# A stack of softmax attention and linear attention on one core: VectorE's exponential by two quadratics, two rings for 4 KB tiles, and an attention order found by looking ahead

## The chip, the core and the metric

The kernel runs on one core of a Trainium2 chip. The core has TensorE (PE, matrix products into the accumulator memory PSUM), VectorE (DVE), ScalarE (ACT), GpSimd (POOL) and SyncE (SP, whose queue issues most DMA transfers). The engines run on their own instruction queues, each in order, and wait for each other by semaphores. Times are device microseconds (us) of the core. The time before is the median of 3 runs, 2476.19 us (2473.14 to 2482.28). A difference under some 0.5% cannot be told from no change.

## The reference, cut to what matters

Four residual layers of 2048 tokens by 512 channels, 32 heads of 16 channels: softmax attention A, linear attention B, and the two again with the same weights.

```python
def _A_ref(x, wqkv, wo):
    qkv = (x @ wqkv).reshape(B, S, 3, H, Dh).transpose(2, 0, 3, 1, 4)
    q, k, v = qkv[0], qkv[1], qkv[2]
    scores = jnp.einsum("bhqd,bhkd->bhqk", q, k) * (Dh ** -0.5)
    p = _softmax(scores, axis=-1)
    o = jnp.einsum("bhqk,bhkd->bhqd", p, v)
    return o.transpose(0, 2, 1, 3).reshape(B, S, D) @ wo

def _B_ref(x, wqkv, w_phi, wo):        # q, k, v as above
    pq, pk = (jnp.einsum("bhsd,hdf->bhsf", t, w_phi) for t in (q, k))
    phi_q, phi_k = (concatenate([_softmax(p), _softmax(-p)], axis=-1) for p in (pq, pk))
    kv, z = jnp.einsum("bhsf,bhsd->bhfd", phi_k, v), jnp.einsum("bhsf->bhf", phi_k)
    o = jnp.einsum("bhqf,bhfd->bhqd", phi_q, kv) / (jnp.einsum("bhqf,bhf->bhq", phi_q, z)[..., None] + 1e-6)
    return o.transpose(0, 2, 1, 3).reshape(B, S, D) @ wo

x = A_x                                  # (1, 2048, 512)
for _ in range(2):
    x = x + _A_ref(_layernorm(x), A_wqkv, A_wo)
    x = x + _B_ref(_layernorm(x), B_wqkv, B_w_phi, B_wo)
```

## The kernel before, in words

*Tiling of attention.* The 32 heads are 8 sets of 4, the 2048 queries 4 blocks of 512; a set and a block are a group G, 32 groups in a layer. A group runs over 16 key tiles of 128 keys. For a key tile and two of the four heads, TensorE computes one score tile of 128 keys by 1024 values (`score_cols`, L1277, 8 matmuls of 49 rows). ScalarE takes the exponential of the whole tile (`scores`, L1284) into an SBUF tile `p` of 4 KB a partition. Two such tiles make a step, and TensorE multiplies them with the values (`pvs`, L1327, 8 matmuls in 32 bits, each profiled as two instructions, over 512 queries, or in two halves of 256). That is 1024 score tiles and 512 steps of P times V in an attention. In PSUM there are two double buffers `s` for ScalarE's tiles; a third double buffer (`double`) and a pair of single ones (`pm`) serve everything else, and one of these two always holds the group's accumulator.

*Power tiles.* Some score tiles get their exponential on VectorE instead (`power_task`). The score goes to `double` or `pm`. For each half of 512 values VectorE evacuates it in two instructions (L1295, L1298: the power of two and the rest), shifts the exponent into place (L1304), squares the rest (L1307) and evaluates a polynomial in four steps (L1309, L1311, L1313, L1315). The result is a tile `px`, of which there is one buffer, so one power tile is in flight.

*Side work.* Between score tiles and P times V, TensorE also makes the next heads' keys, queries and values (`octet`, units of 8 matmuls at L724), the output projection (`part`, `tail`), and in the first attention it prepares the weights of B. VectorE evacuates these (`kq_task`: L1011, L1013, L1016, L1019, L1021; transposes at L985; residual sums at L1361), GpSimd adds, squares (L1108) and subtracts. Query blocks that are done are normalized for the next layer while attention still runs (`stats_task`, L586; `halved`, L609 and L614).

*What sets the order.* `attention` is a planner that runs when the kernel is built. It keeps a clock for TensorE (`pe`) and one for ScalarE (`act`), costs such as 0.217 for a score tile and 0.864 for a step, and times at which buffers come free; tasks of VectorE and GpSimd stand in a list with their own clocks (`Plan`). At each turn it issues a score tile if a buffer `s` is free, else a side unit, else a P times V if a margin allows, else a power tile. The margins come from a table `RULES`, three numbers for each 32 steps. A power tile is aimed 8 steps ahead (`LEAD`) and starts if VectorE's planned work ends within 0.4 us (`VBUSY`). Loads by SP's queue are taken as landed after fixed times (`LAND`, 36 us).

*Buffers.* Tiles of 4 KB: 6 for `p` and 1 for `px` (pool `pp`); 3 `xt` for blocks that DMA loads or stores, and 4 tiles `xn` of 2 KB for normalized rows and the power tile's steps (pool `xp`).

*Layer B.* While the first rows come out of attention's end, B's `feed` projects each 128 tokens, and VectorE takes maximum, minimum, differences and sums of the feature maps (L1717 to L1731). Then `flow`, a second list planner, interleaves B's outputs with the start of the next attention.

## Time and profile before

| what | us |
|---|---|
| median of 3 runs | 2476.2 |
| the profiled execution's span | 2479.1 |
| before the first exponential | 71 |
| first attention | 935 |
| first B: feed, then outputs and the next projections | 168 + 132 |
| second attention | 923 |
| second B: feed, then outputs | 167 + 83 |
| busy: PE, ACT, DVE, POOL | 2307, 2122, 1641, 531 |

The profiled execution has no other time of its own than its span, which is 2.9 us above the median. In a row of groups stand line, engine, operation, output and inputs, shape and count; then busy time in all, the mean of one in ns, and the engine's idle time just before with who ended it. A row of waits gives the one who waited, the one waited for, and then us in all, times, and the longest. A row of a stretch gives its bounds and length, and for each engine its busy us with the number of instructions. A row of the timeline starts with the start and the length. PE's matmuls are pipelined, so the next one starts before the row's length is over.

### The profile page before, as it was taken

Reading aid. Unit: us, or ns where it says so; the run is one execution under the profiler, and the core shown is the slowest. Engines: PE = TensorE matmul, PEld = TensorE weight load, DVE = VectorE, ACT = ScalarE, POOL = GpSimd, SP = SyncE. Lnnn points to the kernel's source line nnn. Section 1 sums busy time; section 2 is a strip of 40 time slices with the busy share of each in tenths; the row PEclk is TensorE's granted clock in tenths of the full one; section 3 lists DMA queues with packets and bytes.
Section 4 is the critical chain, followed back from the end, with each engine's and each line's share of the span. In section 5 each row is a group of like instructions: output and inputs, shape, how many; then the busy total and the mean of one; then the engine's idle time right before and its main releaser. Section 6 shows DMA issues by size and latency. Waiting matters only on the chain.

```text
span 2479.1 us, 110386 instructions
## 1 busy us (share of the span) xinstructions
...
## 2 busy tenths in 40 slices
...
GB/s 193 71 28 8 88 72 37 30 59 55 37 55 155 140 75 67 44 35 18 60 73 57 40 8 63 34 3 53 66 21 42 97 78 43 71 71 26 27 1 112
DMA packets 124025, 143.31 MB, mean 58 GB/s; under 512 B 65193, under 2 KB 70937, under 8 KB 122649
## 3 DMA queue, kind: packets, MB, share of 16 engines
...
q14 instruction: 87, 0.70, 0.1%
...
## 4 chain that ended last, share of the span: by engine, by line
ACT 56%; PE 15%; DVE 13%; issue 12%; POOL 2%; SPq 1%; DMA 1%; POOLq 0%; ACTq 0%; DVEq 0%
ACT p L1284 55%; PE s L1277 3%; PE pm L1327 3%; PE double L1327 1%; PE pbv L1655 1%; DVE su L1728 1%; PE pk L1655 1%; DVE yt L1945 1%; PE pq L1655 1%; PE double L724 1%; DVE f L1720 1%; POOL f L1737 1%; DVE f L1721 1%; SPq L999 1%; DVE mx L1717 1%
## 5 line engine op out<-in xcount | busy, mean ns | idle before, releaser
L1284 ACT ACTIVATE p<-s 128x1024 f32<-128x1024 f32 x1998 | 1838.3, 1077 | 25.1 <-PE s L1277 23.6
L1277 PE MATMUL s<-kq 49*32 49x512 f16 x15104 | 793.4, 382 | 81.4 <-ACT p L1284 61.5
L1327 PE MATMUL pm<-p,v 64*32 64x512 f32 (+1 forms) x13216 | 805.5, 534 | 2.8 <-issue 2.8
L1277 PEld LDWEIGHTS <-kq 49*32 49x32 f16 x15872 | 388.8, 89 | 804.4 <-issue 704.8
L1327 PE MATMUL double<-p,v 64*32 64x512 f32 (+1 forms) x5848 | 320.6, 491 | 0.0
L1327 PEld LDWEIGHTS pm<-p,v 64*32 64x32 f32 x13216 | 262.2, 106 | 42.9 <-issue 7.3
L988 POOL TENSOR_TENSOR yt<-yt,yt 128x512 f32<-128x512 f32 x64 | 85.0, 1327 | 847.2 <-DVE yt L985 822.6
L985 DVE STREAM_TRANSPOSE yt<-pm 128x512 f32<-128x512 f32 x92 | 60.5, 695 | 207.4 <-PE pm L1327 207.4
L1655 PEld LDWEIGHTS <-xnTa 128*128 128x128 f16 x1152 | 111.0, 99 | 155.2 <-DVE f L1721 27.1
L1108 POOL TENSOR_TENSOR sq<-stg 128x512 bf16<-128x512 f16 x48 | 57.2, 1192 | 427.0 <-PE s L1277 266.3
L1737 POOL TENSOR_TENSOR f<-f,su 128x1024 f32<-128x1024 f32 x58 | 112.1, 1933 | 115.7 <-DVE su L1731 103.0
L1327 PEld LDWEIGHTS double<-p,v 64*32 64x32 f32 x5848 | 116.5, 106 | 21.1 <-issue 3.2
L1655 PE MATMUL pbv<-wbv,xnTa 128*128 128x512 f16 x384 | 92.8, 393 | 22.3 <-DVE f L1721 22.3
L1722 ACT ACTIVATE f<-f,c_pB 128x1024 f32<-128x1024 f32 x62 | 70.5, 1148 | 48.2 <-DVE f L1721 48.1
L1011 DVE TENSOR_SCALAR tq<-double,c_qk 128x512 f32<-128x512 f32 x36 | 26.8, 745 | 116.0 <-PE double L724 111.3
L724 PEld LDWEIGHTS <-wA 64*32 64x32 f16 x4608 | 75.5, 93 | 42.4 <-issue 3.6
L1361 DVE SCALAR_TENSOR_TENSOR xt<-pm,c_oA,xt 128x512 f32<-128x512 f32 x56 | 41.8, 746 | 80.5 <-PE pm L724 78.1
L1743 ACT ACTIVATE fk<-f 128x1024 f16<-128x1024 f32 x30 | 31.7, 1057 | 72.5 <-POOL f L1737 72.5
L985 DVE STREAM_TRANSPOSE vyt<-double 128x512 f32<-128x512 f32 x48 | 31.5, 692 | 87.9 <-PE double L724 84.7
L1655 PE MATMUL pq<-wbqk,xnTa 128*128 128x512 f16 x384 | 88.4, 379 | 0.8 <-DVE vt L1682 0.8
L1655 PE MATMUL pk<-wbqk,xnTa 128*128 128x512 f16 x384 | 88.1, 379 | 0.0
L1361 DVE SCALAR_TENSOR_TENSOR xt<-double,c_oA,xt 128x512 f32<-128x512 f32 x56 | 41.8, 746 | 68.2 <-PE double L724 67.6
...
## 6 DMA issues: line engine op xcount, KB each, us to landing
kq<-stg SPq DMA_DIRECT2D x168, 128.0 KB
...
```

The lines of the kernel that those rows point to most:

```text
L724: nc.tensor.matmul(ps[h][c, :], w[r, c], x[r], start=(n == 0), stop=(n == of - 1), skip_group_check=True)
L985: nc.vector.transpose(ys[u].rearrange("p a b -> p (a b)"), ps[u])
L988: nc.gpsimd.tensor_tensor(ys[0], ys[0], ys[1], ALU.add)
L1108: nc.gpsimd.tensor_tensor(sq, hi, hi, ALU.mult)
L1277: nc.tensor.matmul(banks2[u][32 * c:32 * c + 32, :], self.side(g, half, 64 * u, 0, kt * P + 32 * c, 32), self.side(g, half, 64 * u, 1, j * ...
L1284: nc.scalar.activation(pt, s, AF.Exp, scale=EXPS)
L1327: nc.tensor.matmul(acc[h][32 * hh:32 * hh + 32, part], self.oct[o]["v"][r, x:x + 32], pt[r, hh % 2, part], start=(kt == 0), stop=(kt == NT ...
L1361: nc.vector.scalar_tensor_tensor(xt[:, u, :], ps[h], con["oA"], xt[:, u, :], op0=ALU.mult, op1=ALU.add)
L1655: nc.tensor.matmul(dst, xnT[:, a, c, t * P:(t + 1) * P], w(b, c), start=(i == 0 and c == 0), stop=(i == 2 and c == NC4 - 1))
L1722: nc.scalar.activation(f, f, AF.Exp, scale=con["pB"])
L1737: nc.gpsimd.tensor_tensor(f3, f3, self.part_sums(f3, slice(0, 64), factor), ALU.mult)
L1743: nc.scalar.activation(fk[:, 0, :], ff, AF.Copy)
```

## The change: what it does

1. *Power tiles.* One instruction evacuates the score (two for the single banks `pm`) as an integer whose bits are a floating-point number; two integer instructions split it into a mantissa and a power of two; four instructions evaluate two quadratics and multiply them in. All work on 1024 values at once: 7 or 8 instructions instead of 16. Two power tiles may be in flight.
2. *Rings.* Pool `pp` has 9 tiles of 4 KB that compute alone uses (`p`, the power tile's two helpers, normalized rows two at a time); pool `xp` has 3 for DMA's blocks, which a power tile's result also uses when one is free. The planner books both.
3. *Order.* The table is gone. Where a score tile, a P times V, a half of one, a side unit or waiting are open, `look` searches all sequences over the next 2.6 us for the least time lost by ScalarE. Power tiles are taken as soon as buffers and VectorE's plan (3.0 us) allow, 7 steps ahead, or 10 if one is in flight.
4. *SP's queue.* Every DMA start adds a cost to a clock `sp`; loads count as landed by it.
5. *Keys and queries.* One clamp on VectorE (L1019) is left out, and GpSimd's square is started after the subtraction.

```diff
-VBUSY = 0.4
-RULES = (((2, 0.05, 0.01), (2, 0.05, 0.05), (2, 0.15, 0.0), (2, 0.15, 0.2), (2, 0.15, 0.0), (1, 0.15, 0.0), (2, 0.02, 0.1), (1, 0.02, 0.0),
...
-LEAD = 8
+LEAD = 7
+MORE = 10
+IDLE = 0.5
+AHEAD_US = 2.6
+SENT = 36.0, 28.0
+RING4 = 9
+OUTER = 3
+VBUSY = 3.0
...
-    pp = pool("pp", bufs=6)
+    pp = pool("pp", bufs=RING4)
+    xp = pool("xp", bufs=OUTER)
...
+    def send(dst, src, cost=0.62):
+        nc.sync.dma_start(dst, src)
+        if state["layer"] is not None:
+            state["layer"].sends(cost)
...
-            xn = xp.tile([P, D], F32, tag="xn", name="xn", bufs=4)
+            if t // 2 not in self.xn2:
+                self.xn2[t // 2] = pp.tile([P, 2, D], F32, tag="p", name="xn")
+            xn = self.xn2[t // 2][:, t % 2, :]
...
             nc.vector.tensor_scalar(hi, tq, CLAMP, -CLAMP, op0=ALU.min, op1=ALU.max)
-            self.spawn(self.square_task(hi, sqs), self.plan.end - self.plan.now + 0.15)
-            yield "V", 0.43
-            nc.vector.tensor_scalar(tq, tq, CLAMP, -CLAMP, op0=ALU.min, op1=ALU.max)
             yield "V", 0.7
             nc.vector.tensor_tensor(lo, tq, hi, ALU.subtract)
+            self.spawn(self.square_task(hi, sqs), self.plan.end - self.plan.now + 0.15)
...
-        def power_task(self, G, kt, half, idx, ps):
...
+        def power_task(self, G, kt, half, idx, ps, outer):
+            pt = xp.tile([P, 2, 512], F32, tag="xt", name="px") if outer else pp.tile([P, 2, 512], F32, tag="p", name="px")
+            m = pp.tile([P, 2, 512], F32, tag="p", name="pm")
+            t = pp.tile([P, 2, 512], F32, tag="p", name="pz")
+            yi = pt.bitcast(I32)
+            if idx:
+                for u in range(2):
+                    yield "V", 0.7, 0
+                    nc.vector.tensor_scalar(yi[:, u], ps[u], 8192.0, FIELD * 2.0 ** 23, op0=ALU.mult, op1=ALU.add)
+            else:
+                yield "V", 1.2, 0
+                nc.vector.tensor_scalar(yi, self.pair, 8192.0, FIELD * 2.0 ** 23, op0=ALU.mult, op1=ALU.add)
             self.freed(idx)
...
+            nc.vector.tensor_scalar(m.bitcast(I32), yi, KEEP, LEADM, op0=ALU.bitwise_and, op1=ALU.bitwise_or)
+            nc.vector.tensor_scalar(yi, yi, POWER, LEADE, op0=ALU.bitwise_and, op1=ALU.bitwise_or)
+            nc.vector.scalar_tensor_tensor(t, m, PA, m, op0=ALU.add, op1=ALU.mult)
+            nc.vector.scalar_tensor_tensor(pt, t, PB, pt, op0=ALU.add, op1=ALU.mult)
+            nc.vector.scalar_tensor_tensor(t, m, PC, m, op0=ALU.add, op1=ALU.mult)
+            nc.vector.scalar_tensor_tensor(pt, t, PD, pt, op0=ALU.add, op1=ALU.mult)
...
+            self.busy -= 1
+            self.give(n=2)
...
+            def look(pe, act, ea, eb, si, vi, cut, held, slots, cost, until, best, side):
...
+                if nxt is not None and free <= pe and slots:
+                    start = max(act, pe + THERE, slots[0])
+                    gone = max(0.0, start - act)
...
+                        best, pick = got, "S"
+                if ready <= pe:
...
+                        best, pick = got, "V"
...
+            def wants(pe):
+                if not tiles or sum(x <= pe for x in slots) < 2 + KEEP_POWER + (sum(x <= pe for x in self.outers) <= WITHHELD) or plan.clock["V"] > pe + VBUSY or not pvq:
+                    return False
...
+                    if wants(pe) and min(self.pfree) <= pe:
+                        G, kt = aim()
+                        power.add((G, kt, 1))
+                        self.busy += 1
+                        far = sum(x <= pe for x in self.outers) > WITHHELD and not self.closed
+                        self.grab(1, self.outers if far else slots)
+                        self.grab(2)
```

The change moves instructions. On ScalarE, around the first attention, the order before (`p<-s` is the exponential of a score tile, `sq` and `v` belong to the first heads' keys and values, `f` to B's feature maps):

```order
L1110 ACTIVATE sq<-stg 128x512
L1103 ACTIVATE v_162<-pv__797 128x16x32
L1110 ACTIVATE sq<-stg 128x512 x2
L1103 ACTIVATE v_162<-pv__905 128x16x32
L1284 ACTIVATE p<-s 128x1024 x1002
L1722 ACTIVATE f<-f,c_pB 128x1024 x2
```

and now:

```order
L1156 ACTIVATE sq<-stg 128x512
L1149 ACTIVATE v_162<-pv__789 128x16x32
L1156 ACTIVATE sq<-stg 128x512 x2
L1149 ACTIVATE v_162<-pv__897 128x16x32
L1334 ACTIVATE p<-s 128x1024 x980
L1841 ACTIVATE f<-f,c_pB 128x1024 x2
```

22 exponentials are gone from the first attention; in the second one the count goes from 996 to 970, and all other rows of ScalarE stand as they stood.

On VectorE, a power tile early in the first attention. Before, the evacuation and the first of two halves (`pw` is the rest, `pz` its square):

```order
L1295 TENSOR_SCALAR px<-double 128x512
L1298 SCALAR_TENSOR_TENSOR pw<-px,double 128x512
L1295 TENSOR_SCALAR px<-double 128x512
L1298 SCALAR_TENSOR_TENSOR pw<-px,double 128x512
L1304 TENSOR_SCALAR px<-px 128x512
L1307 TENSOR_TENSOR pz<-pw 128x512
L1309 SCALAR_TENSOR_TENSOR px<-pz,px 128x512
L1311 SCALAR_TENSOR_TENSOR pz<-pw,pz 128x512
L1313 SCALAR_TENSOR_TENSOR px<-pz,px 128x512
L1315 SCALAR_TENSOR_TENSOR px<-pw,px 128x512
```

and now a whole one (`pm` is the mantissa, `pz` the quadratic; `rec` and `yn` belong to the division of a finished group):

```order
L1349 TENSOR_SCALAR px<-double 128x1024
L1106 TENSOR_SCALAR rec<-yt_2680 128x16
L1352 TENSOR_SCALAR pm<-px 128x1024
L1108 RECIPROCAL rec<-rec 128x16
L1354 TENSOR_SCALAR px<-px 128x1024
L1113 TENSOR_TENSOR yn<-yt_2680,rec 128x16x16
L1356 SCALAR_TENSOR_TENSOR pz<-pm 128x1024
L1358 SCALAR_TENSOR_TENSOR px<-pz,px 128x1024
L1360 SCALAR_TENSOR_TENSOR pz<-pm 128x1024
L1362 SCALAR_TENSOR_TENSOR px<-pz,px 128x1024
```

The sixteen instructions of 512 values have become seven of 1024, and the accumulator bank is read in the first one alone.

On VectorE at the end of the first attention. Before (`xnTa_2` is query block 2 for B, `mx`, `mn` and `f` are B's feed, the rest is the division of the last group):

```order
L609 CAST xnTa_2_23496<-double 128x4x128
L614 TENSOR_TENSOR xnTa_2_23496<-double,xnTa_2_23496 128x4x128
L1060 TENSOR_SCALAR rec<-yt_24311 128x16
L1717 TENSOR_REDUCE mx<-pk 128x32
L1062 RECIPROCAL rec<-rec 128x16
L1718 TENSOR_REDUCE mn<-pk 128x32
L1067 TENSOR_TENSOR yn<-yt_24311,rec 128x16x16
L1720 TENSOR_TENSOR f<-pk,mx 128x32x16
L1076 STREAM_TRANSPOSE yb<-yn 128x512
L1721 TENSOR_TENSOR f<-mn,pk 128x32x16
L1079 CAST osp<-yb 128x512
L1717 TENSOR_REDUCE mx<-pq 128x32
```

and now, from the same reciprocal's first row on:

```order
L1106 TENSOR_SCALAR rec<-yt_24844 128x16
L619 TENSOR_SCALAR xn<-xt,mv,ly 128x512
L1108 RECIPROCAL rec<-rec 128x16
L619 TENSOR_SCALAR xn<-xt,mv,ly 128x512
L1113 TENSOR_TENSOR yn<-yt_24844,rec 128x16x16
L1839 TENSOR_TENSOR f<-pk,mx 128x32x16
L1122 STREAM_TRANSPOSE yb<-yn 128x512
L1840 TENSOR_TENSOR f<-mn,pk 128x32x16
L1125 CAST osp<-yb 128x512
L642 CAST xnTa_2_24137<-pm_24862 128x4x128
L1836 TENSOR_REDUCE mx<-pq 128x32
L647 TENSOR_TENSOR xnTa_2_24137<-pm_24862,xnTa_2_24137 128x4x128
```

Two normalizations (L619, before L586) and, here and just behind, two pairs of cast and subtraction (L642 and L647, before L609 and L614) have moved from before the feed's first `mx<-pk` to after it, with three small steps of the normalization's square root.

463 lines of the change are left out of this document (265 added, 198 removed), and 3 rows, old and new, of the table RULES.

## The prediction

> **What bounds the kernel now.** I read the page first (its chain of waits), then the stages, then the exponentials alone.
>
> ```profile
> span 2479.1 us, 110386 instructions
> ACT 56%; PE 15%; DVE 13%; issue 12%; POOL 2%; SPq 1%; DMA 1%; POOLq 0%; ACTq 0%; DVEq 0%
> ```
>
> More than half of the chain that ended last is ScalarE. The next view gives the busy time of each engine by stage: first attention, the feed of the hedgehog layer behind it, second attention, its feed.
>
> ```profile
> core 0: us, PE busy (x) PEld busy (x) DVE busy (x) ACT busy (x) POOL busy (x), PEclk, DMA share, GB/s
> 71.00:1006.00 935.00, 891.26 (x22800) 437.59 (x22808) 540.24 (x1000) 922.04 (x1002) 113.05 (x107) 1.00 0.28 64
> 1006.00:1174.00 168.00, 153.72 (x1065) 80.36 (x1049) 153.23 (x243) 76.20 (x96) 99.38 (x104) 0.99 0.06 21
> 1306.00:2229.00 923.00, 878.87 (x23425) 434.70 (x23425) 557.28 (x980) 916.03 (x996) 111.21 (x103) 1.00 0.23 50
> 2229.00:2396.00 167.00, 154.31 (x1057) 80.73 (x1041) 152.20 (x242) 75.87 (x95) 99.05 (x102) 0.98 0.06 20
> ```
>
> The two attentions are 1858 us of the span, and in them ScalarE stands idle for 13.0 and 7.0 us only. In the feeds VectorE is the full engine (153 of 168 us). The lines of the exponential, from the groups and from the waits of ScalarE in the two attentions:
>
> ```profile
> L1284 ACT ACTIVATE p<-s 128x1024 f32<-128x1024 f32 x1998 | 1838.3, 1077 | 25.1 <-PE s L1277 23.6
> ACT p L1284 <- PE s L1277: 13.2, 22, 3.9
> ACT p L1284 <- PE s L1277: 10.4, 9, 5.0
> ```
>
> All of ScalarE's work in attention is this one instruction: 922.04 us / 1002 and 916.03 / 996 are both 0.920 us apiece (the 1077 ns of one overlap with the next). The time of an attention is the number of exponentials by 0.920 us, plus waits for the scores. So the change is first a question of how many exponentials are left.
>
> **The change part by part.** *Exponentials.* The order of ScalarE is the same before and after but for one number in each attention: 1002 becomes 980, and 996 becomes 970. 48 tiles move to VectorE (50 there become 98): 48 x 0.920 = **-44.2 us** (20.2 and 23.9), as long as nothing else ends last there.
>
> *VectorE's tile.* Its rows now, and the rows that are nearest to the new ones:
>
> ```profile
> L1295 DVE TENSOR_SCALAR px<-double 128x512 f32<-128x512 f32 x74 | 50.4, 681 | 9.8 <-PE double L1277 9.8
> L1298 DVE SCALAR_TENSOR_TENSOR pw<-px,double 128x512 f32<-128x512 f32 x74 | 50.5, 682 | 1.8
> L1304 DVE TENSOR_SCALAR px<-px 128x512 int32<-128x512 int32 x100 | 42.4, 424 | 0.0
> L1307 DVE TENSOR_TENSOR pz<-pw 128x512 f32<-128x512 f32 x100 | 68.2, 682 | 0.0
> L1309 DVE SCALAR_TENSOR_TENSOR px<-pz,px 128x512 f32<-128x512 f32 x100 | 70.3, 703 | 2.9
> L1311 DVE SCALAR_TENSOR_TENSOR pz<-pw,pz 128x512 f32<-128x512 f32 x100 | 72.5, 725 | 2.8
> L1313 DVE SCALAR_TENSOR_TENSOR px<-pz,px 128x512 f32<-128x512 f32 x100 | 71.8, 718 | 2.8
> L1315 DVE SCALAR_TENSOR_TENSOR px<-pw,px 128x512 f32<-128x512 f32 x100 | 72.6, 726 | 3.0
> L1990 DVE SCALAR_TENSOR_TENSOR xt<-fl,c_oB,xt 128x1024 f32<-128x1024 f32 x13 | 16.3, 1260 | 5.1 <-PE fl L1987 5.1
> L614 DVE TENSOR_TENSOR xnT<-pst,xnT 128x1024 f16<-128x1024 f32 x6 | 7.1, 1218 | 0.6 <-ACT xnT L611 0.6
> L614 DVE TENSOR_TENSOR xnTa<-double,xnTa 128x512 f16<-128x512 f32 x12 | 8.3, 692 | 0.4
> ```
>
> Old tile: two halves of 0.681 + 0.682 + 0.424 + 0.682 + 0.703 + 0.725 + 0.718 + 0.726, 10.68 us, one in flight. New: the two L614 rows say that 512 more elements cost 0.526 us. Four two-input steps of 1024 then take between 1.218 and 1.260; I take 1.24, 4.96 in all. Two integer steps of 1024 lie between 0.424 (no more than now) and 0.848 (twice the row); only half the 0.526 goes on top if they go on at the rate of L1304, 0.68 each, 1.36. The evacuation is 2 x 0.681 or one of about 1.22; 1.3. Sum 7.6 us. VectorE gets 98 x 7.6 - 50 x 10.68 = +211 us.
>
> It also loses an instruction per key or query block (L1019), and its subtraction L1021 no longer starts beside GpSimd's square, which now follows it:
>
> ```profile
> L1019 DVE TENSOR_SCALAR tq<-tq 128x512 f32<-128x512 f32 x48 | 20.9, 435 | 1.2
> L1021 DVE TENSOR_TENSOR stg<-tq,stg 128x512 f16<-128x512 f32 x48 | 54.1, 1128 | 0.9
> L1108 POOL TENSOR_TENSOR sq<-stg 128x512 bf16<-128x512 f16 x48 | 57.2, 1192 | 427.0 <-PE s L1277 266.3 <-DVE stg L1016 76.4 <-PE double L1277 51.1
> ```
>
> That is -21 us, and up to 48 x (1.128 - 0.682) = -21 more. So VectorE goes from 1097 busy us in the two attentions to about 1265 of 1815, 70%: hidden behind ScalarE on average, but every evacuation now queues behind steps of 1.24 us instead of 0.72.
>
> L1021 at 1.128 us against 0.682 for L1307, of the same size, is what GpSimd beside VectorE costs here. The Trainium skill (GPSIMD Engine Reference, Key points) has the rule that speaks against the change: GpSimd shares its SBUF interfaces with VectorE, which contends in two-port modes or with two SBUF inputs, and after the evacuation every step of the new tile is one of those. The trace agrees in L1021. By it 98 x 4.96 us, a factor of 1.65 while GpSimd runs (12% of the first attention), would add 38 us of VectorE time; by the rows of L1309 to L1315, which carry the same exposure at 0.70 to 0.73, it is 3%, 15 us. Either is off ScalarE's path, so the sum is the same by both; it weighs on the slower rival alone.
>
> *TensorE's order.* Its work is the same but for 114 more of the P times V steps that go in two halves of 256 queries, each half with its own weight loads (328 instead of 214, counted in the order). A stretch of TensorE in the first attention gives the prices:
>
> ```profile
> 131.53 0.41 PE L1277 MATMUL s<-kq 49*32 49x512 f16 x8
> 131.75 0.84 PE L724 MATMUL double<-xnT,wA 64*32 64x512 f16 x24
> 132.45 0.41 PE L1277 MATMUL s<-kq 49*32 49x512 f16 x8
> 132.66 1.06 PE L1327 MATMUL pm<-p,v 64*32 64x512 f32 x16
> 133.52 0.41 PE L1277 MATMUL s<-kq 49*32 49x512 f16 x8
> ```
>
> From start to start a score tile takes 0.22, three side units 0.70, a step of P times V 0.86. An attention has 1024, 612 and 512 of them: 225 + 143 + 440 = 808 us, and I allow 40 for transposes and folds. ScalarE's floor after the change is 980 x 0.920 = 902 and 892, so TensorE has 6% left and does not become the bound on average. The row of TensorE's busy time says otherwise: 891 of 935 us leaves 2.6% against the new 915. The Trainium skill (Perfetto Trace Analysis, Identifying the Most-Contended Engine) holds matmul busy time a bad measure and takes the weight loads' instead; these are 438 of 935 us here, far from full. The starts above agree with it.
>
> *Waits of ScalarE.* The new order is searched 2.6 us ahead, the queue of SP is counted, and power tiles take ring buffers from the exponentials. What that does to the 20 us of waits the trace cannot show. Below: all gone, -20. Above: each of the 48 added tiles costs one wait as long as TensorE's longest ordinary one, 0.5 us, +24.
>
> ```profile
> PE s L1277 <- ACT p L1284: 29.8, 83, 0.5
> PE double L1277 <- DVE tq L1013: 1.5, 1, 1.5
> ```
>
> I take **+2**, the middle; waits of TensorE for VectorE were as rare as the second row with 22 tiles, which speaks for the lower half, and the fuller VectorE for the upper.
>
> *What falls behind the first attention.* The order on VectorE there now has two normalizations (L586), three small steps and two pairs of cast and subtraction (L609, L614) of query block 2 after the first `mx<-pk`, where VectorE is full. Before, these lay under the exponentials:
>
> ```profile
> 999.00 0.68 DVE L609 CAST xnTa<-double 128x512 f16<-128x512 f32 x1
> 999.72 0.69 DVE L614 TENSOR_TENSOR xnTa<-double,xnTa 128x512 f16<-128x512 f32 x1
> 1000.32 0.15 DVE L571 TENSOR_TENSOR lu<-ly 128x2 f32<-128x2 f32 x1
> 1000.51 0.16 DVE L572 TENSOR_TENSOR lu<-lu 128x2 f32<-128x2 f32 x1
> 1002.68 1.00 DVE L586 TENSOR_SCALAR xn<-xt,mv,ly 128x512 f32<-128x512 f32 x2
> ```
>
> 2 x 1.32 + 1.0 + 3 x 0.19 = 4.2 us; they delay the first `mx<-pq`, so every later row of that queue. Bounds 0 (the feed has 15 idle us) and 4.2; **+3.5**. Behind the second attention a reciprocal and a product go the other way: **-0.5**.
>
> *Nothing else.* The tiles of normalization in the 4 KB ring, the extra buffers in the hedgehog layers and the start up to 71 us keep their orders; ScalarE's rows there are the same one by one. I cost them at nothing; what hides them is VectorE's own queue in the feeds.
>
> Sum: -44.2 + 2 + 3.5 - 0.5 = -39.2 on the profiled 2479.1 us: 2439.9. This execution lies 2.9 us above the median of the runs, 2476.2, so **2437**.
>
> **The rivals.**
> *The search removes the waits too.* The lone stalls (3.9 and 5.0 us) and many small ones go: -20 instead of +2, 2415. For it: the old order decides greedily. Against: part of the stalls is named "issue" on TensorE, which no order of the work is sure to remove.
> *TensorE follows only in part.* By its busy rows it is nearly full; then half of the 44.2 comes back as waits for `s`: 2437 + 22 = 2459.
> *The buffers tie ScalarE to VectorE.* 193 exponentials now carry a wait on VectorE, because their ring buffer last held a step of a power tile; before, 2 did. If each costs 0.2 us (a sixth of a 1.24 us step), 39 us return: 2476, no change. Against: the planner books these buffers from the end of the tile on.
> *Slower: power tiles come late.* The queue of TensorE is in order. A P times V that waits for a late `px` holds up the score tiles queued behind it, and ScalarE starves after the 0.36 us (29.8 / 83) by which TensorE runs ahead. A tile late by one step of VectorE costs 1.24 - 0.36 = 0.88 us. The net gain of 39 is gone from 44 late tiles of 98, and at 60 late the time is 2437 + 53 = 2490. For it: two tiles in flight share VectorE with every evacuation, and GpSimd stretches them. Against: VectorE stands idle for 30% of the time.
>
> **How the numbers follow.** Chances: forecast 0.50, waits removed 0.15, TensorE in part 0.17, buffers 0.10, late tiles 0.08. The range is -44.2 + 0 - 0.5 - 20 = -65 to -44.2 + 4.2 + 24 = -16 on the median: 2411 to 2460; to hold the case of TensorE in part I set 2412 to 2463, which leaves the last two out. A change under 0.5% (12 us) cannot be told from none here; faster takes the first three cases, 0.82, no change 0.10, slower 0.08.
>
> **What would show it.** In the changed profile: 1950 exponentials and about 1794 us busy; attentions of some 917 and 900 us; idle time before the exponential under 45 us; 1024-wide steps of VectorE at 1.22 to 1.26, integer ones near 0.68; the feed behind the first attention at 170 to 172 us, the second at 167. Wrong would be: idle time of ScalarE over 50 us (by releaser: scores that waited for `px` or for evacuations is the slower rival, VectorE itself the buffers), an integer step at 0.85 or more, or 0.920 us apiece that has grown.

## The result, and the profile after

The changed kernel takes 2495.03 us (median of 6 runs, 2492.27 to 2501.25), the kernel before beside it 2479.24 us (6 runs, 2473.14 to 2488.24). The ratio is 1.0067, 95% interval 1.0046 to 1.0089: slower by some 16 us. The forecast was 2437 us. All runs behind these times had a granted TensorE clock of 0.97 to 0.99; one further execution, the profiled one of old_less_pe below, had 0.32 and took 7824 us, so that kernel has a time but no profile to read.

First the head of the changed kernel's page, span and chain:

```profile
span 2490.5 us, 114010 instructions
ACT 38%; DVE 25%; PE 22%; issue 11%; POOL 2%; DMA 1%; SPq 0%; ACTq 0%; POOLq 0%; DVEq 0%
```

ScalarE has gone from 56% of the chain to 38%, VectorE from 13% to 25%, TensorE from 15% to 22%. ScalarE has less work, and more of the chain now goes through VectorE and TensorE. The same four stretches as before (first attention, feed, second attention, feed):

```profile
core 0: us, PE busy (x) PEld busy (x) DVE busy (x) ACT busy (x) POOL busy (x), PEclk, DMA share, GB/s
71.50:1000.20 928.70, 879.63 (x24016) 459.02 (x24020) 625.40 (x942) 906.86 (x980) 133.93 (x107) 1.00 0.28 65
1000.20:1170.20 170.00, 154.61 (x1065) 80.77 (x1053) 155.33 (x252) 75.77 (x95) 99.39 (x104) 0.99 0.07 23
1304.80:2236.30 931.50, 876.33 (x24032) 455.03 (x24029) 653.23 (x914) 897.03 (x970) 129.45 (x103) 0.99 0.23 50
2236.30:2403.30 167.00, 153.97 (x1043) 80.44 (x1040) 150.58 (x239) 75.17 (x94) 98.13 (x102) 0.98 0.06 20
```

With the bounds of the profile before taken to a tenth (71.0, 1006.1, 1174, 1306.1, 2228.5, 2396) the parts of the span changed by: head +0.5, first attention -6.4, feed +2.1, the rest of the first B +2.5, second attention +9.1, feed -0.5, the rest of the second B +4.1. That is the +11.4 us of the two spans. The attentions, from which 44 us were to come, are together 2.7 us longer.

ScalarE's exponential in the whole page, then what it waited for in each attention:

```profile
L1334 ACT ACTIVATE p<-s 128x1024 f32<-128x1024 f32 x1950 | 1803.9, 1069 | 61.7 <-PE s L1327 37.6
ACT p L1334 <- PE s L1327: 12.8, 22, 1.7
ACT p L1334 <- DVE pz L1360: 5.1, 5, 1.9
ACT p L1334 <- DVE px L1362: 2.0, 4, 1.1
ACT p L1334 <- PE s L1327: 24.7, 20, 8.8
ACT p L1334 <- DVE pz L1360: 7.7, 6, 1.9
ACT p L1334 <- DVE px L1362: 3.0, 5, 1.5
ACT p L1334 <- DVE rec L1106: 2.6, 2, 2.0
```

From the stretches, ScalarE's idle time in the attentions is 928.7 - 906.86 + 931.5 - 897.03 = 56.3 us; before, by those bounds, it was 19.4. Its busy time fell by 34.2 (1838.1 to 1803.9, 0.925 us apiece instead of 0.920). So 34.2 us of work went and 36.9 us of waiting came. The new waits by the rows: 17.8 us directly for VectorE's `pz` and `px` (none before), 2.6 for `rec`, and for scores 37.5 against 23.6. Of the last, one wait is 8.8 us. Here are that place's rows, VectorE, GpSimd, TensorE and ScalarE in the order of their starts:

```profile
1951.01 1.22 DVE L1349 TENSOR_SCALAR px<-double 128x1024 int32<-128x1024 f32 x1
1951.58 0.38 POOL L1088 PARTITION_ALL_REDUCE nma<-nmx  x1 [5.83 <-DVE px L1362]
1959.87 0.26 POOL L1092 TENSOR_SCALAR okt<-nma 1x1 f32<-1x1 f32 x1 [7.51 <-issue]
1960.16 0.15 DVE L2396 TENSOR_REDUCE lowest<-okt 1x1 f32<-1x8 f32 x1 [7.93 <-POOL okt L1092]
1962.11 1.20 DVE L1349 TENSOR_SCALAR px<-double 128x1024 int32<-128x1024 f32 x1
1963.37 1.48 PE L757 MATMUL double<-woA,ob 64*32 64x512 f16 x24 [8.02 <-DVE px L1349]
1965.40 1.02 ACT L1334 ACTIVATE p<-s 128x1024 f32<-128x1024 f32 x1 [8.80 <-PE s L1327]
```

`lowest` (L2396) is the check at the end of the program that decides whether a fallback must run. It needs nothing but the last `okt`. In VectorE's order it stands right behind an evacuation, ahead of the rest of that power tile. From the start of GpSimd's reduction to `okt` it takes 8.3 us. VectorE waits 7.93, with the next evacuation behind it, TensorE 8.02 for the PSUM pair that it frees, ScalarE 8.80 for the score behind that. From 1959 to 1967 us the granted TensorE clock is 0.57, and the 24 matmuls of the row at 1963.37 take 1.48 us, where 24 of that shape take 0.84 in the prediction's stretch. Before, the check stood behind the last step of a finished power tile, and VectorE had no evacuation to make until 2 us later:

```profile
1903.44 0.15 DVE L2275 TENSOR_REDUCE lowest<-okt 1x1 f32<-1x8 f32 x1 [3.42 <-POOL okt L1046]
```

The last view is VectorE's power tile in groups, with GpSimd's addition:

```profile
L1362 DVE SCALAR_TENSOR_TENSOR px<-pz,px 128x1024 f32<-128x1024 f32 x98 | 127.8, 1304 | 1.3
L1356 DVE SCALAR_TENSOR_TENSOR pz<-pm 128x1024 f32<-128x1024 f32 x98 | 124.0, 1266 | 0.1
L1358 DVE SCALAR_TENSOR_TENSOR px<-pz,px 128x1024 f32<-128x1024 f32 x98 | 123.7, 1263 | 1.1
L1360 DVE SCALAR_TENSOR_TENSOR pz<-pm 128x1024 f32<-128x1024 f32 x98 | 123.2, 1258 | 1.2
L1352 DVE TENSOR_SCALAR pm<-px 128x1024 int32<-128x1024 int32 x98 | 73.9, 755 | 3.9
L1354 DVE TENSOR_SCALAR px<-px 128x1024 int32<-128x1024 int32 x98 | 71.3, 728 | 1.2
L1349 DVE TENSOR_SCALAR px<-double 128x1024 int32<-128x1024 f32 x54 | 65.7, 1216 | 13.1 <-PE double L1327 12.9
L1036 POOL TENSOR_TENSOR yt<-yt,yt 128x512 f32<-128x512 f32 x64 | 101.2, 1581 | 832.5 <-DVE yt L1033 805.2 <-DMA v<-vyt 8.8 <-DVE sBv_mm L376 8.0
```

The four steps sum to 5.09 us, the two integer steps to 1.48, the evacuation to some 1.28 (54 times 1.216, 44 times 2 x 0.682): 7.86 us a tile, where 7.6 was forecast.

### The profile page after: what moved, and what is told of

It reads as the page before. It is cut to its first block, busy times and chain, and to the rows that moved or that the text cites. A ratio compares the mean times of both kernels' runs of the same rounds, so it can differ in the third digit from the quotient of the medians.

```text
span 2490.5 us, 114010 instructions
## 1 busy us (share of the span) xinstructions
PE 2303.2 (92%) x51946; PEld 1194.6 (48%) x51946; DVE 1824.6 (73%) x2796; ACT 2086.7 (84%) x2328; POOL 570.3 (23%) x644
## 4 chain that ended last, share of the span: by engine, by line
ACT 38%; DVE 25%; PE 22%; issue 11%; POOL 2%; DMA 1%; SPq 0%; ACTq 0%; POOLq 0%; DVEq 0%
ACT p L1334 37%; PE s L1327 5%; PE pm L1376 4%; PE double L1376 4%; PE double L757 2%; DVE pz L1360 2%; DVE su L1847 1%; DVE pz L1356 1%; DVE px L1362 1%; DVE yt L1033 1%; PE pbv L1774 1%; PE pm L757 1%; DVE px L1358 1%; PE pk L1774 1%; DVE yt L2064 1%
## 5 line engine op out<-in xcount | busy, mean ns | idle before, releaser
L1334 ACT ACTIVATE p<-s 128x1024 f32<-128x1024 f32 x1950 | 1803.9, 1069 | 61.7 <-PE s L1327 37.6
L1327 PE MATMUL s<-kq 49*32 49x512 f16 x14744 | 779.2, 381 | 85.4 <-ACT p L1334 67.0
L1376 PE MATMUL pm<-p,v 64*32 64x512 f32 (+1 forms) x10392 | 596.9, 494 | 0.4 <-issue 0.4
L1376 PE MATMUL double<-p,v 64*32 64x256 f32 (+1 forms) x10048 | 560.8, 483 | 4.3 <-DVE rec L1106 1.6
L1036 POOL TENSOR_TENSOR yt<-yt,yt 128x512 f32<-128x512 f32 x64 | 101.2, 1581 | 832.5 <-DVE yt L1033 805.2
L1376 PEld LDWEIGHTS pm<-p,v 64*32 64x32 f32 x10392 | 213.0, 106 | 43.8 <-issue 5.7
L1376 PEld LDWEIGHTS double<-p,v 64*32 64x32 f32 x10048 | 206.2, 106 | 45.9 <-issue 7.2
L1154 POOL TENSOR_TENSOR sq<-stg 128x512 bf16<-128x512 f16 x48 | 65.2, 1358 | 354.9 <-PE s L1327 168.4
L1362 DVE SCALAR_TENSOR_TENSOR px<-pz,px 128x1024 f32<-128x1024 f32 x98 | 127.8, 1304 | 1.3
L1358 DVE SCALAR_TENSOR_TENSOR px<-pz,px 128x1024 f32<-128x1024 f32 x98 | 123.7, 1263 | 1.1
L1360 DVE SCALAR_TENSOR_TENSOR pz<-pm 128x1024 f32<-128x1024 f32 x98 | 123.2, 1258 | 1.2
L1356 DVE SCALAR_TENSOR_TENSOR pz<-pm 128x1024 f32<-128x1024 f32 x98 | 124.0, 1266 | 0.1
L1841 ACT ACTIVATE f<-f,c_pB 128x1024 f32<-128x1024 f32 x62 | 70.2, 1148 | 51.4 <-DVE f L1840 51.1
L1414 DVE SCALAR_TENSOR_TENSOR xt<-pm,c_oA,xt 128x512 f32<-128x512 f32 x58 | 43.4, 749 | 88.7 <-PE pm L757 86.2
L1414 DVE SCALAR_TENSOR_TENSOR xt<-double,c_oA,xt 128x512 f32<-128x512 f32 x54 | 40.5, 749 | 89.5 <-PE double L757 88.9
L757 PEld LDWEIGHTS <-wA 64*32 64x32 f16 x4608 | 75.8, 93 | 41.0 <-issue 1.4
```

The source lines that it names most:

```text
L757: nc.tensor.matmul(ps[h][c, :], w[r, c], x[r], start=(n == 0), stop=(n == of - 1), skip_group_check=True)
L1036: nc.gpsimd.tensor_tensor(ys[0], ys[0], ys[1], ALU.add)
L1327: nc.tensor.matmul(banks2[u][32 * c:32 * c + 32, :], self.side(g, half, 64 * u, 0, kt * P + 32 * c, 32), self.side(g, half, 64 * u, 1, j * ...
L1334: nc.scalar.activation(pt, s, AF.Exp, scale=EXPS)
L1356: nc.vector.scalar_tensor_tensor(t, m, PA, m, op0=ALU.add, op1=ALU.mult)
L1358: nc.vector.scalar_tensor_tensor(pt, t, PB, pt, op0=ALU.add, op1=ALU.mult)
```

## The experiments

Unless said otherwise a kernel is the changed one with the edit shown. "Attentions" is the sum of the two, "idle" ScalarE's idle time in them, both from the stretches as above. For the kernel before they are 1857.5 and 19.4 us. Each length of an attention comes from one profiled execution, which can lie up to 7 us from the median of its kernel. In the changed kernel, check_late and mixed, ScalarE, VectorE and GpSimd do the first attention in the same order, and it took 928.7, 928.3 and 930.4 us: a difference of 2 or 3 us between attentions says nothing.

Some expectations count ScalarE's lost time "over 0.905 each": the length of the attentions less 0.905 us for each exponential. Exponentials that follow without a stop start 0.903 to 0.905 us apart (801 of the 1949 spacings of the changed kernel). The idle time shows less than what is lost, since the records of neighbours overlap and a short stop only shortens the overlap. By this measure the kernel before loses 49 us and the changed one 95.

| kernel | power tiles | attentions | idle | ratio to before, 95% interval |
|---|---|---|---|---|
| before | 50 | 1857.5 | 19.4 | 1 |
| changed | 98 | 1860.2 | 56.3 | 1.0067 (1.0046 to 1.0089) |
| check_late | 98 | 1852.9 | 49.9 | 1.0025 (1.0012 to 1.0038) |
| late_true | 82 | 1885.5 | 67.7 | 1.0284 (1.0266 to 1.0302) |
| late_release | 93 | 1858.5 | 51.1 | 1.0087 (1.0071 to 1.0102) |
| one_flight | 77 | 1852.3 | 33.7 | 1.0001 (0.9991 to 1.0012) |
| two_80 | 80 | 1852.3 | 35.0 | 1.0023 (1.0013 to 1.0033) |
| mixed | 89 | 1846.5 | 37.6 | 0.9994 (0.9984 to 1.0004) |
| parted | 93 | 1853.0 | 36.0 | 0.9984 (0.9972 to 0.9995) |
| parted_one | 82 | 1857.0 | 30.0 | 1.0022 (1.0011 to 1.0033) |
| fewer_halves | 81 | 1858.3 | 38.4 | 1.0020 (1.0007 to 1.0032) |
| no_power | 0 | 1908.4 | 24.3 | 1.0197 (1.0177 to 1.0217) |
| old_no_power | 0 | 1900.5 | 17.2 | 1.0184 (1.0167 to 1.0202) |
| arith_only | 48 | 1856.5 | 17.2 | 1.0076 (1.0057 to 1.0095) |

### The one instruction that blocks VectorE

```diff
                 plan.now = FAR / 2
                 plan.advance(FAR)
+                if self.li == 1:
+                    nc.vector.tensor_reduce(lowest, okt[0:1], AX.X, ALU.min)
+                    nc.vector.tensor_scalar(flag, lowest, shmin, None, op0=ALU.is_lt)
...
-    with tc.manual_schedule(engines=COMPUTE):
-        nc.vector.tensor_reduce(lowest, okt[0:1], AX.X, ALU.min)
-        nc.vector.tensor_scalar(flag, lowest, shmin, None, op0=ALU.is_lt)
```

> The changed kernel with one edit: the two small VectorE instructions that read the shift table for the final branch (lowest, flag) stand at the end of the second attention's work instead of where they stand now, directly behind the first instruction of a power tile. In the changed kernel's trace VectorE waits there 7.9 us for GpSimd's okt, the power tile behind it stops with a PSUM pair in hand, TensorE waits 8.0 us for that pair and ScalarE 8.8 us for scores. Theory A (this one blocked instruction costs what ScalarE loses there): the time falls by 8 to 10 us, to about 2486, the second attention from 931.5 to about 922, and the waits of the exponentials on 'PE s' from 37.6 us to about 28. Theory B (the loss is caught up elsewhere, since TensorE or VectorE sets the pace): within 3 us of the changed kernel.

Measured 2485.09 us. The ratio went from 1.0067 to 1.0025, 10 us, and the second attention from 931.5 to 924.6. Theory A holds for the time. The waits on scores fell to 32.2 us only and not to 28, and 2.4 us of the gain lie behind the second attention. All edits below but those of no_power and of the kernels called old and arith_only contain this one.

### What the power tiles are worth

Without any, in the new order (`POWERS = 0`) and in the old:

> The changed kernel without any power tile: ScalarE computes all 2048 exponentials, with the changed rings and the changed order. It measures what 98 power tiles are worth here. By ScalarE alone it is 98 x 0.92 = 90 us more than the changed kernel, 2585, if power tiles cost ScalarE nothing. Theory A (power tiles cost ScalarE waits: pz and px 17.8 us, late scores behind VectorE 9 us and more): the waits of the exponentials fall from 61.7 us to below 30, and the time is only 2545 to 2560. Theory B (the waits belong to TensorE's new order): the waits stay above 45 us and the time is 2575 or more.

> The kernel before without any power tile: all 2048 exponentials on ScalarE, old rings, old order. With no_power (changed rings and order, no power tile either, attentions 958.7 and 949.8 us, 2532 in all) it shows what the rings and the look-ahead do by themselves, and what the first 50 power tiles were worth. By ScalarE alone the 50 tiles are worth 50 x 0.92 = 46 us: 2481 + 46 = 2527. Theory A (rings and look-ahead change nothing by themselves, the loss comes with the power tiles): attentions within 5 us of no_power's, time 2522 to 2537. Theory B (the new order itself loses on ScalarE): attentions together 10 us or more below no_power's 1908.5, time below 2520.

The two attentions of no_power, then of old_no_power:

```profile
71.30:1029.90 958.60, 892.38 (x23488) 451.59 (x23488) 309.35 (x627) 942.00 (x1024) 115.33 (x107) 1.00 0.27 63
1331.20:2281.00 949.80, 878.24 (x23104) 434.17 (x23104) 258.62 (x510) 942.07 (x1024) 113.90 (x103) 1.00 0.23 49
71.60:1023.30 951.70, 894.39 (x22304) 427.41 (x22304) 332.78 (x650) 942.26 (x1024) 110.92 (x107) 1.00 0.27 63
1324.50:2273.30 948.80, 888.16 (x23072) 429.89 (x23071) 286.85 (x534) 941.00 (x1024) 107.64 (x103) 1.00 0.22 49
```

Times 2532.15 and 2528.28 us. For no_power theory A holds for the waits (29.8 us before the exponential in the whole page), and the time is even lower than A said. For old_no_power the time is A's, but its attentions are 7.9 us shorter than no_power's, between A's 5 and B's 10. By the times the two kernels differ by 0.13% only, some 3 us, and the intervals overlap. So the rings and the search lose 3 to 8 us by themselves, and that they lose anything is not clear of the noise. In the old order 50 power tiles shortened the attentions from 1900.5 to 1857.5, 0.86 us each, nearly the full 0.92. From there to check_late 48 more bring 4.6 us, 0.1 each, or up to 12.5 us, 0.26 each, if the 7.9 of the new order are counted apart. By the times they bring nothing: check_late is 0.25% slower than the kernel before.

One at a time, and 80 with two at a time:

```diff
-                if not tiles or sum(x <= pe for x in slots) < 2 + KEEP_POWER + ...
+                if not tiles or self.busy or sum(x <= pe for x in slots) < 2 + KEEP_POWER + ...    # one_flight
...
-KEEP_POWER = 1
+KEEP_POWER = 2                                                                                     # two_80
```

> check_late with one more edit: a power tile is begun only when no other one is under way in the plan. It places 77 power tiles instead of 98 (ScalarE 1971 exponentials, 21 more, +19.3 us at 0.92). Theory A (the last power tiles are worth little, because each of them puts VectorE's queue behind its plan): exponentials' idle time falls from 55.3 us to about 40 and the time is within 5 us of check_late (2485). Theory B (each power tile saves ScalarE its 0.92 us): 19 us slower than check_late, 2504.

> check_late, and a power tile is begun only when one buffer of the ring more is free (KEEP_POWER 2 instead of 1); two may still be under way. 80 power tiles, about as many as with one at a time (77), ScalarE 1968 exponentials. In one_flight the exponentials lost 68.6 us over 0.905 each, and 6.0 us of it to pz and px; in check_late (98 tiles, two under way) 88.0 and 17.3. Theory A (the number of power tiles sets the waits): like one_flight, 66 to 72 us over 0.905, pz and px below 9 us, about 2480. Theory B (two under way at once set them, since the helpers of both are held twice as long): pz and px 12 us or more, 78 us or more over 0.905, 2490 or more.

Measured 2479.66 and 2485.22 us. The groups of check_late, one_flight and two_80 and, below, the attentions of one_flight:

```profile
L1334 ACT ACTIVATE p<-s 128x1024 f32<-128x1024 f32 x1950 | 1803.0, 1069 | 55.3 <-PE s L1327 32.2
L1334 ACT ACTIVATE p<-s 128x1024 f32<-128x1024 f32 x1971 | 1818.7, 1072 | 39.0 <-PE s L1327 30.3
L1334 ACT ACTIVATE p<-s 128x1024 f32<-128x1024 f32 x1968 | 1817.3, 1072 | 40.7 <-PE s L1327 34.5
...
71.10:1012.20 941.10, 886.75 (x24016) 460.63 (x24016) 546.66 (x865) 916.89 (x992) 122.40 (x107) 1.00 0.28 64
1314.30:2225.50 911.20, 869.96 (x23952) 451.53 (x23950) 588.68 (x842) 901.76 (x979) 127.68 (x103) 1.00 0.23 51
```

In both the direct waits for `pz` and `px` fell from 17.3 us to 6.0 and 3.8. Two at once are not needed for that (two_80's theory A for the waits; its time is 5 us above A's). But two_80 also asks for one more free buffer, and the number of tiles does not set these waits alone: further down, parted has 93 tiles, two at once, and 6.9 us of them, fewer_halves 81 tiles, one at a time, and 11.1. The reading that matters is the sum of the attentions: 98, 80 and 77 tiles give 1852.9, 1852.3 and 1852.3 us. The other kernels of the new order with 81 to 93 tiles, late_true aside, lie between 1846.5 and 1858.5 and follow no line. Within these few us, what ScalarE is spared beyond some 77 tiles it spends waiting. One_flight's theory A holds for the time.

The two orders put together, two at a time in the first attention and one in the second (`self.li and self.busy`):

> check_late, and a power tile is begun only when no other is under way in the plan, in the second attention alone; the first keeps two under way. 89 power tiles (44 and 45), ScalarE 1959 exponentials. It puts together what the runs showed apart: check_late's first attention took 928.2 us (one at a time: 941.2), one_flight's second 911.2 us (two at a time: 924.6). Theory A (each attention's order is worth by itself what it was worth there): 71.8 + 928 + 304.6 + 911 + 251.5 = 2467 us, about 12 us faster than the kernel before. Theory B (an order's stalls depend on how the run came to it, and do not carry over): 2478 to 2486, as one_flight and check_late.

Measured 2477.41 us, half a us below theory B's range and 10 above A's sum. The first attention came as before (930.4), the second 4.9 us longer than in one_flight, the stretches around them 2.5 us longer than A's sum. By this one profile, about two thirds of the 13 us that one_flight had gained in its second attention carried over.

### Buffers and planned durations

```diff
-            yield "V", 0.62, 2          # integer steps        late_true
+            yield "V", 0.74, 2
...
-            yield "V", 1.16, 2          # the four steps
+            yield "V", 1.27, 2
...
-            self.give(n=2)              # helpers come free    late_release
+            self.give(1.6, 2)
```

> The same move of the two check instructions, and the planner is told the durations that the changed kernel's trace shows for a power tile: 0.74 instead of 0.62 us for the two integer steps, 1.27 instead of 1.16 for the four floating ones, 1.22 and 0.69 for the evacuation; a tile is planned at 7.78 us instead of 7.08. With them it places 82 power tiles instead of 98, so ScalarE computes 1966 exponentials, 16 more. Theory A (buffers come free later than planned, because planned costs are short): the exponentials' waits on VectorE (pz 12.8 and px 5.0 us in the changed kernel) fall below 5 us; against check_late that is -13 of waits and +16 x 0.92 = +14.7 of exponentials, so within 5 us of check_late, and a kernel about 10 us faster than the changed one. Theory B (the ring is too short whatever is planned): the waits on pz and px stay above 12 us, and the time is 10 to 15 us above check_late.

> check_late with one more edit: the planner counts the two helper buffers of a power tile (pm, pz) as free 1.6 us after its planned last instruction instead of 0.1 us, so an exponential is given one of them later or another buffer. Nothing else is told; it places 93 power tiles instead of 98 (ScalarE 1955 exponentials, 5 more, +4.6 us). In check_late's trace the exponentials wait 12.3 us for pz and 5.0 us for px. Theory A (the buffers come free later than planned, and ScalarE, which works in order, stands behind them): those 17.3 us fall below 5, and with 5 exponentials more the two attentions are together 8 us shorter or more (check_late 928.2 + 924.6 = 1852.8); the time is 2470 to 2480. Theory B (whatever is late on VectorE is paid by ScalarE or TensorE in another place): the waits on pz and px go, the waits on 'PE s' (32.2 us) grow by as much, and the attentions stay within 4 us of check_late.

Measured 2552.64 and 2503.43 us: neither theory of either. Late_true's waits on `pz` and `px` fell from 17.3 to 12.0 us only, and other places lost more: the attentions are 33 us longer, where 16 exponentials more explain 15, and there are 24 us behind the first attention, 19 behind the second, and a stop of VectorE in the first attention that is the check's over again, with another engine. VectorE's rows:

```profile
372.08 1.23 DVE L1349 TENSOR_SCALAR px<-double 128x1024 int32<-128x1024 f32 x1 [8.22 <-DMA dF<-bf]
```

The result of the power tile went into a buffer of DMA's ring from which a store was still under way; VectorE stood 8.22 us, TensorE 7.93 for the pair. And the stretch behind the first attention is 328.6 us instead of check_late's 304.5, where residual sums of the output projection (L1414) and normalizations stand on VectorE behind the last exponential: ScalarE's first instruction of the feed waits 31.5 us for VectorE (`ACT f L1844 <- DVE f L1843: 36.2, 3, 31.5` in the waits of that stretch). In late_release `pz` still costs 11.6 us, and the stretch behind the second attention is 13 us longer than check_late's. The planner books buffers as a number of free ones; which buffer an exponential gets is decided later, so a later booking does not keep it from a particular one. Whether a ring of their own for the helpers would end these waits was not tried.

### TensorE's halves

`PARTED`, what the search is charged for cutting a step of P times V in two, was 0.05. Parted sets 1.0, parted_one the same with one power tile at a time, fewer_halves 0.12 with one at a time. By TensorE's instruction counts (16 more for each step that is cut) 328 steps are cut in the changed kernel, 322 in one_flight, 147 in fewer_halves, none in the parted kernels. (The expectations count cuts in other units, and not both in the same.)

> check_late, and the look-ahead is charged 1.0 us instead of 0.05 for cutting a value product into halves, so that it cuts none (the changed kernel has about 1450 instruction groups of 256 columns, this one has none; 93 power tiles, ScalarE 1955 exponentials). Theory A (the halves cost TensorE instructions and the scores come late behind them: of ScalarE's lost time in check_late about 15 us stand behind a TensorE that was busy and 12 behind gaps that no engine explains): these fall by 10 us or more, and the time is 2475 or less. Theory B (the halves let scores pass a value product, and pay for themselves): ScalarE's lost time over 0.905 each grows from 88.0 us, and the time is above 2490.

> parted (no value product cut into halves) and one power tile at a time in both attentions. 82 power tiles, ScalarE 1966 exponentials, 11 more than parted (+10 us at 0.92). Alone the one edit brought 6.6 us against check_late (parted, 2478.5) and the other 5.4 us (one_flight, 2479.7). Theory A (two separate losses: halves leave TensorE gaps that no engine explains, and two power tiles at once tie ScalarE's buffers to VectorE): the gains add, 2470 to 2475, the exponentials' idle time from parted's 41.4 us to about 30. Theory B (both edits remove the same loss, or without halves a score waits behind a whole value product and the tiles given up are paid in full): 2477 to 2488.

> one_flight, and a cut into halves is charged 0.12 us instead of 0.05: 1149 instruction groups of 256 columns instead of about 1530, 81 power tiles instead of 77, ScalarE 1967 exponentials. Theory A (the cuts that gain least in the plan cost more on the chip than they gain): ScalarE's lost time over 0.905 each falls below one_flight's 68.6 us and the time is 2470 to 2477. Theory B (cuts cost nothing by themselves; what parted gained came from another order): within 4 us of one_flight, 2476 to 2484.

Measured 2478.47, 2485.91 and 2484.76 us. TensorE's waits that no engine explains (the rows `<- issue`) sum to 7.5 us in check_late and 0.2 in parted. But they do not go by the number of cuts: the changed kernel has 4.7 us with check_late's 328 cuts, fewer_halves 8.7 with 147, and parted_one 2.5 with none.

Parted's own profile holds neither theory: these gaps go, but the attentions are as long as check_late's with 5 power tiles fewer. ScalarE is busy 0.929 us per exponential there and not 0.925, although one record has become shorter (median 1046 ns against 1080): the records overlap less, and waiting that was idle time in check_late is part of that. Its time is 0.16% under the kernel before, and of the kernels that leave no work out it is the only one whose interval lies below 1. As the best of eleven orders, run in one series, it may owe that to luck. With one at a time the gain is gone, and fewer cuts bring nothing either (5 us above one_flight): theory B for parted_one, and a little worse than B for fewer_halves. Theory B of parted_one had two causes, one loss that both edits remove or power tiles given up at full price; the runs do not tell them apart.

### The new arithmetic in the old order

```diff
-                nc.vector.tensor_scalar(y, ps[u], OFF, MAGIC, op0=ALU.add, op1=ALU.add)
+                nc.vector.tensor_scalar(yi[:, u], ps[u], 8192.0, FIELD * 2.0 ** 23, op0=ALU.mult, op1=ALU.add)
...                                    # two integer steps and four others on each half, in the old ring
```

> The kernel before with one part of the change alone: the power tile is computed by the two quadratics (in halves of 512 columns, in the old ring of four 2 KB tiles), everything else as before: old rings, old order, about as many power tiles (48 instead of 50, ScalarE 2000 exponentials). If the old order is bound by ScalarE and its few power tiles are set by the rules of the order, cheaper VectorE work changes nothing: 2479 plus 2 x 0.92, so 2477 to 2484. If VectorE's work held ScalarE up before, it is faster than 2474. A power tile should cost VectorE about 8.6 us (6 x 0.69 + 2 x 0.68 ... by halves: 2 x (0.68 + 2 x 0.42 + 4 x 0.70)) instead of 10.7.

Measured 2500.01 us, slower, though VectorE has 104 us less to do in the attentions. The attentions did as forecast (1856.5). The loss is 15.4 us between them, and 15.0 of it lie in the feed: from the last exponential to the start of its last feature map it is 182.1 us, before 167.1. ScalarE's first instruction of the feed accounts for 5.6: it waits 13.7 us (before: 8.1), and on VectorE three residual sums and more of a query block's normalization now stand between the last exponential and it. Where the other 9 arise was not followed.

```profile
ACT f L1717 <- DVE lu L565: 13.7, 1, 13.7
ACT f L1722 <- DVE f L1721: 10.1, 3, 8.1
```

The first row is arith_only's, the second that of the kernel before. So an edit of the planner's costs also moves what is left over at an attention's end: in this kernel, late_true and late_release 13 to 24 us hang on it.

### Whose work sets the length

Six kernels keep the order of the instructions and leave out work. Less_pe leaves out 3 of the 12 products of each projection, less_act computes 64 exponentials of an attention over half their width (the value products then read the first half twice), less_both does both, all in check_late's order. The three with old_ do the same in the order of the kernel before.

```diff
-                mm_cols(ps, w(i), x(i), i, of)
+                if of != 12 or i not in (5, 6, 7):                             # less_pe
+                    mm_cols(ps, w(i), x(i), i, of)
...
-            nc.scalar.activation(pt, s, AF.Exp, scale=EXPS)
+            n = 1 if half == 0 and kt % 8 == 3 else 2                          # less_act
+            nc.scalar.activation(pt[:, :n], s[:, :n], AF.Exp, scale=EXPS)
```

> The kernel before, in its own order, with 3 of the 12 products left out of each projection in the attentions (36 projections x 3 x 0.217 us = 23.4 us of TensorE's work in each attention, 47 in all; keys, queries and values lose their low parts). Theory A (ScalarE sets the length of the attentions before, as the prediction took it): the two attentions lose less than 8 us of 1857.6. Theory B (TensorE sets it): they lose 30 us or more. In between: both do, in turn.

> The kernel before, in its own order, with 64 exponentials of each attention computed over 512 of their 1024 columns (the value products read the first half twice): about 64 x 0.43 = 27 us of ScalarE's work less in each attention, 55 in all. Theory A (ScalarE sets it): the two attentions lose 40 us or more. Theory B (TensorE sets it): less than 15.

> check_late (98 power tiles, new order) with the same 23.4 us of TensorE's work left out of each attention. Theory A (ScalarE's lost time has its cause in VectorE and the buffers): less than 10 us of 1852.8 lost. Theory B (with 98 tiles TensorE is the engine that is always late, and the scores behind it): 25 us or more.

> check_late with the same 64 exponentials of each attention at half width, about 55 us of ScalarE's work less. Theory A (ScalarE sets it): the attentions lose 40 us or more of 1852.8. Theory B (they no longer follow ScalarE, which is why 98 tiles bring no more than 77): less than 20 us. The same slope as in the kernel before would say that the loss lies in each order's waits and not in another bound.

> The kernel before with both edits: 3 of 12 products of each projection left out, and 64 exponentials of each attention at half width. Alone they brought 6.2 and 7.4 us, 13.6 together. Theory A (TensorE's floor and ScalarE's floor both lie just under the present length, each hides the other): 25 us or more faster than the kernel before, 2455 or less. Theory B (something else, fixed in the order, sets the length): 14 us or less, 2466 or more.

> check_late (98 power tiles, new order) with both edits. Alone they brought 4.9 and 6.5 us, 11.4 together. Theory A: 25 us or more faster than check_late's 2485, 2460 or less. Theory B: 12 us or less, 2473 or more; then the lost time of the new order, on VectorE's buffers (20 us in less_act) and on TensorE's gaps, stays whatever the two engines do.

| left out | time, before's order | attentions | time, check_late's order | attentions |
|---|---|---|---|---|
| nothing | 1 | 1857.5 | 1.0025 | 1852.9 |
| TensorE's | 0.9978 (0.9965 to 0.9991) | no profile | 1.0002 (0.9987 to 1.0017) | 1850.4 |
| ScalarE's | 0.9971 (0.9957 to 0.9986) | 1845.4 | 0.9997 (0.9983 to 1.0011) | 1852.8 |
| both | 0.9932 (0.9914 to 0.9951) | 1838.2 | 0.9975 (0.9963 to 0.9987) | 1841.2 |

Each of the four single edits gave back little: by the times 5 to 7 us, less than a quarter of what was left out. So the theories that one engine alone sets the length fail on both sides: less TensorE work speaks against TensorE (theory A of both, for old_less_pe by its time alone), less ScalarE work against ScalarE (theory B of both). ScalarE's groups in old_less_act show what was taken away, by shape, and the two attentions below them what came of it:

```profile
L1285 ACT ACTIVATE p<-s 128x1024 f32<-128x1024 f32 x1870 | 1744.9, 1057 | 41.8 <-PE s L1277 23.5 <-ACT p L1285 0.3
L1285 ACT ACTIVATE p<-s 128x512 f32<-128x512 f32 x128 | 82.7, 646 | 1.3 <-PE s L1277 1.1
...
71.20:999.80 928.60, 887.06 (x22800) 432.53 (x22808) 540.28 (x1000) 907.66 (x1002) 113.22 (x107) 1.00 0.28 65
1298.80:2215.60 916.80, 874.49 (x23409) 433.21 (x23415) 556.92 (x980) 900.17 (x996) 111.27 (x103) 1.00 0.23 50
```

An exponential of 512 columns takes 0.41 us less than a full one, 53 us in all. ScalarE's busy time in the attentions fell by 30 us only (922.1 + 916.0 to 907.7 + 900.2), because the neighbours' records now overlap by 252 us in all and not by 313, so that short stops count as busy. Of these 30 the attentions gave back 12 in the old order, and 7 by the times. In check_late's order 35 were spared and the profile shows nothing back, but less_act's profiled execution is the slowest of its ten, 6.7 us above their median; by the times it is 7 us there too. A stretch of TensorE in old_less_act shows how the rest is lost:

```profile
509.34 0.41 PE L1277 MATMUL s<-kq 49*32 49x512 f16 x8
509.56 0.63 PE L724 MATMUL double<-xnT,wAv 64*32 64x512 f16 x16
510.09 0.41 PE L1277 MATMUL s<-kq 49*32 49x512 f16 x8
510.31 0.84 PE L724 MATMUL double<-xnT,wAv 64*32 64x512 f16 x24
511.01 0.41 PE L1277 MATMUL s<-kq 49*32 49x512 f16 x8
511.23 1.05 PE L1328 MATMUL pm<-p,v 64*32 64x512 f32 x16
512.09 0.41 PE L1277 MATMUL s<-kq 49*32 49x512 f16 x8
```

No row has idle time ahead of it. The scores start 0.75, 0.92 and 1.08 us apart, because that is how long the work takes that the order put between them. Over three they average 0.92, ScalarE's own pace. ScalarE starts a short exponential at 512.63 here, the next one at 513.38 and the one after it at 514.47: 0.76 us are followed by 1.08, and the two take 1.84, as long as two full ones. It is so at all 128 places: behind a short one the next two start 0.77 and 1.06 us apart on average, 1.83 together, where the kernel before has 0.94 and 0.93, 1.87 together. In less_act it is 0.91 and 1.04 against check_late's 1.02 and 0.95. So a shorter exponential only waits for the next score (shown for these places). TensorE is full here, and elsewhere it waits for ScalarE (63.9 us of `PE s` waiting for `p` in the kernel before, 71.1 in the changed one). So I read the two engines as setting the pace in turn, over stretches of a few microseconds; that is a reading of one stretch, and the sums do not prove it. Both edits together bring 17 us in the old order, where the single ones add up to 13, and 12 in check_late's, where they add up to 13; the difference of 4 lies within the intervals. That is theory B for check_late and between the theories for the kernel before. In check_late two thirds of the 35 us that ScalarE was spared did not come out even then; that part hangs on waits between the engines, VectorE's buffers among them (21.0 us of `pz` and `px` in less_act). What share each has there stays open.

## Why the prediction was wrong

*The step that failed* is the first of the sum, "48 x 0.920 = -44.2, as long as nothing else ends last there", with "TensorE has 6% left and does not become the bound on average". The exponentials were counted right (1950, 1803.9 us busy against 1794 forecast), so ScalarE's work did fall by 34 us. But an exponential was not worth its length on the path any more: 36.9 us of waiting came in its place, and the attentions are 2.7 us longer. The price was taken from ScalarE's small idle time, 20 us in 1858. Leaving out 30 us of ScalarE's work from the same kernel in its own order gave back 12, and 7 by the times (shown). A share near 98% said that ScalarE was nearly always working; it did not say that scores would come any faster. For that the prediction looked at TensorE's average, and the average came out: TensorE is busy 1756.0 of the 1860.2 us, so it has 5.6% left. An average does not decide it: at the 128 shortened places ScalarE got the scores hardly sooner (two spacings of 1.83 us instead of 1.87). The first 50 power tiles had been worth 0.86 us each, while TensorE's idle time in the attentions fell from 118 to 88 us; the prediction carried that price on to where it no longer held. With 98 tiles TensorE's idle time is 104 us again, so a full TensorE is not the whole cause. Which waits make up the rest stays open.

*The waits of ScalarE* were put at +2 with bounds of -20 to +24; they rose by 36.9. 8.8 of it is one instruction, the check, which stands in VectorE's order right behind an evacuation: the prediction walked the order for what fell behind the attention and not for instructions of VectorE that wait for GpSimd. Moving it gave some 10 us (shown). 17.8 are waits for buffers that a power tile held, 20 of them of 0.9 us, where the rival "buffers" had put 193 of 0.2. That rival had the mechanism and half the size. What these waits cost the attentions is not shown: one_flight and two_80 removed 11 and 13 of check_late's 17.3 us, but they also gave 21 and 18 exponentials back to ScalarE, and the attentions stayed.

*The slower rival* was late `px`, TensorE standing before P times V. It did not come: no matmul waited for the last step of a power tile, and the weight loads before P times V waited for it twice, 0.5 us in all. What TensorE did wait for was the first step, the evacuation that frees the pair, 9.3 us in the row of L757, 8.0 of them through the check.

*TensorE follows only in part* (2459, 0.17) was the nearest in mechanism: half of the gain was to come back as waits for scores. All of it came back, but only 13.9 of the 36.9 us as waits for scores, and 8.8 of these are the check.

*VectorE's tile*: forecast 7.6 us, measured 7.86; the integer steps at 0.755 and 0.728 against 0.68, the others at 1.26 to 1.30 against 1.24. The subtraction (L1021, now L1066) came down from 1.128 to 0.865 us and not to 0.682. VectorE's busy time in the attentions, 1278.6 us, against 1265. The Trainium skill (GPSIMD Engine Reference, Key points) says that GpSimd shares its SBUF interfaces with VectorE and contends with VectorE's instructions that have two SBUF inputs or run in a two-port mode. The rows agree: with the new tiles GpSimd's addition takes 1581 ns, before 1327, and without power tiles in the new order 1325. Of the 64 additions 27 run beside a two-input step of a power tile and take 1925 ns, the others 1330; before it was 9 of 64, at 1558 and 1290.

*The feeds*: +3.5 and -0.5 forecast, +2.1 and -0.5 measured; right. "Nothing else" was short by 6.6 us in the later parts of B. In check_late all that lies behind the second attention is 1.2 us longer than before, against 3.6 in the changed kernel, with the two instructions of the check moved and the same order otherwise. It was not followed up.

*The sign.* Of the 16 us lost to the kernel before, some 10 are the check (shown). Without it the attentions are 4.6 us shorter than before's, where 44 were forecast. If the rings and the search lose the 7.9 us by which the two kernels without power tiles differ in their profiles, the 48 tiles more bring 12.5; by the times that loss is 3 and within the noise. The stretches outside are 6.5 us longer than before's (2481.0 - 1852.9 against 2479.1 - 1857.5). A further 3 us of the miss are the base: with six runs the kernel before takes 2479.2 us, and the prediction started from the 2476.2 of three.
